# A spectral mixing layer and a two-layer MLP on one core: the PReLU addition one step later, a new step table, another DMA order on GpSimd, and seven-product down blocks in 18 blocks for 21

## The chip, the core and the metric

The kernel runs on one core of a Trainium2 chip. The metric is the device time of one execution in microseconds (us). Engines are named as the profile names them: PE multiplies matrices, PEld is its weight load, DVE is the vector engine, ACT the scalar engine, POOL is GpSimd (it issues part of the DMAs), SP issues the other DMAs.

## The reference

```python
X = np.fft.rfft(x, axis=1)                     # x: 8 batches x 3008 tokens x 256
y = np.fft.irfft(X * (filt_r + 1j * filt_i)[None], n=3008, axis=1)
x = y.reshape(24064, 256)
h = x @ w_in                                   # 256 -> 2048
g = np.maximum(h, 0.0) + alpha * np.minimum(h, 0.0)
out = g @ w_out                                # 2048 -> 256
```

A filter in the frequency domain mixes the tokens of each batch; then every token goes through a two-layer MLP with a PReLU whose slope is given per hidden unit.

## The kernel before, in words

**The transform.** 3008 is 47 x 64. Each batch's transform is made of four kinds of pieces, all matmuls on PE in float16. `piece_a` (16 per batch, L209) is the first stage over 47; its results are evicted into `asb`, a buffer of 384 KB (two of them), and every fourth piece saves one to a scratch tensor in DRAM (`a_dram`, L214, on SP). `turn_a` (L221, SP) loads it back transposed as `at`. `piece_b` (12 per batch, each a pair of frequencies, L229) is the second stage, and DVE multiplies its PSUM result by two forms of the filter, `ww` (with `filts_s`, L232) and `uu` (with `filt_s`, L233); a pair of DMAs on POOL (L235) adds `ww` into `uu` with the two halves of the partitions exchanged. `piece_c` (12, L247) starts the inverse from `uu`; its results go out to `v_dram` and come back as `zt` (L256, L265, SP). `piece_d` (16, L272) ends the inverse and is evicted into `yT`, where the MLP reads it. Batch zero has its own form of these pieces (class First) without the detours through DRAM, and it runs mostly before the steps begin; its last pieces are `piece_t` and `piece_d`. All the transform's PSUM results share two banks, `psF0` and `psF1`, in an order that the string BANKS writes out.

**The MLP.** The 24064 tokens are cut into 48 blocks (512 tokens, every twelfth-from-sixth 384). A block has 16 **steps**; step 16n + j is step j of block n. In a step, `up` (L497) makes one of 16 slices of the hidden layer: two matmuls into half of a two-bank PSUM tile `hps`, of which there are two. In each odd step the tile is full: ACT copies it into `gtb` (L505, 128 x 1024), DVE makes min(g, 0) times (alpha - 1) in two instructions (L508, into `m`), and adds `m` to `gtb` (L509). `gtb` has room for two blocks.

**The down product** of a block follows its up products by LAG steps, interleaved with the next blocks' ups: `while todo and done < (step - LAG) / 16` draws its matmuls. It has two forms. `eight` (L534) is the plain product: 64 matmuls of 256 columns for 512 tokens, evicted by ACT (L539). `seven` (L556), for the blocks in FAST, is a Strassen-Winograd product of 2 x 2 blocks: 112 matmuls of 128 columns. It needs sums of parts of `g`, made in two halves each (`sums`): w = 1 and w = 2 on DVE into `ss` (L517, L519), w = 3 and w = 4 as adding DMAs on POOL within `gtb` (L521, `gtb<-gtb`) and from `ss` (L523, `gtb<-ss`); SUMS and TAIL give the steps, counted from the block's first. It has five evictions on ACT and two additions on DVE (L476, through the list `late`). Combinations of `w_out` for it are made once (`combine`, STEPS_K).

**The order.** No scheduler moves anything: each engine runs its instructions in the order in which the program issues them, and semaphores hold it where data or buffers are missing. The tables say at which step a piece is issued, in steps from a batch's origin, 96 (b - 1): STEPS_A to STEPS_D for batches four to seven, FIRST for batches one to three, STEPS_T and STEPS_E for the rest of batch zero, STEPS_X for loading x of batches two and three, STEPS_N for the four negations of `filt_s` (`neg`, L623). A step number so orders the instructions of one engine; an engine that has nothing to wait for runs ahead of the others. Within a step come: the late additions and stores, the sums, the planned pieces, `up`, and the down matmuls that are due.

**POOL's queue at the opening** (L434 to L441): w_out in two DMAs, x of batch one in eight, one copy of `twi_s`, two copies of half of `filt_s` into `filts_s` (768 KB each), and then batch two's x as its step and its buffers allow.

Of the kernel before, what the change touches and what calls it, by code (L numbers as in the profile page):

```python
# [19 lines left out]
DFF = 2048  # L20
NH = 32
BANKS = (
    "010101010101010101010101010101001010010110010010101010101010101010110101101010101010101011010101"
    "010101010101010101010110110101001011010101011010110111010010101010101010010110100010101110101101"
    "010010101100101010010101010101010101001101010101010010110111010110101010101010101010101010101001"
    "010101010100101101101010010101010101010101010101010101100101101010110100100010100101010101010101"
    "01010101010101101010101101001110101010101010101010101010"
)
STEPS_A = (-84, -81, -77, -76, -65, -59, -58, -58, -56, -53, -52, -51, -50, -48, -46, -43)
STEPS_B = (-21, -15, 4, 6, 13, 21, 25, 27, 32, 40, 54, 55)  # L30
STEPS_C = (2, 10, 16, 19, 24, 33, 35, 46, 62, 63, 70, 70)
STEPS_D = (89, 89, 90, 91, 92, 94, 95, 98, 100, 101, 105, 113, 118, 125, 144, 147)
STEPS_T = (0, 0, 2, 2, 13, 17, 19, 21, 21, 35, 40, 43)
STEPS_E = (6, 6, 7, 11, 23, 27, 29, 29, 53, 54, 55, 56)
STEPS_N = (24, 29, 35, 37)
STEPS_K = (118, 121, 128, 133, 143)
STEPS_X = ((20, 27, 42, 52), (107, 109, 113, 126))
FIRST = (
# [12 lines left out]
)  # L51
FAST = frozenset((8, 10, 12, 14, 16, 18, 20, 22, 24, 26, 28, 30, 32, 34, 36, 38, 40, 42, 43, 44, 45))
SUMS = ((9, 1, 0), (10, 3, 0), (16, 2, 0), (17, 1, 1), (17, 3, 1), (19, 2, 1), (20, 4, 0), (21, 4, 1))
TAIL = ((12, 1, 0), (12, 3, 0), (18, 1, 1), (18, 3, 1), (18, 2, 0), (18, 2, 1), (20, 4, 0), (21, 4, 1))
LAG = 16
AF = mybir.ActivationFunctionType
OP = mybir.AluOpType

# [41 lines left out]
def kernel(  # L100
# [10 lines left out]
    nc = tc.nc  # L111
# [30 lines left out]
    twi_s = konst.tile([128, NK1, 128], FP16, name="twi_s")  # L142
    filt_s = konst.tile([128, NK1, D], FP16, name="filt_s")
    filts_s = konst.tile([128, NK1, D], FP16, name="filts_s")
# [12 lines left out]
    twx_s = tw_s.rearrange("p a k c -> p (a k) c")[:, 0:NK1]  # L157
    yT = konst.tile([128, 2, 2 * NFFT], FP16, name="yT")

    def xrow(b, h, c):  # L160
        return bass.AP(tensor=x.tensor, offset=x.offset + (b * NFFT + NH * h + 8 * c) * D,
                       ap=[[N2 * D, N1], [1, 8 * D]])

    def load_x(b, c):
        xs = p_x.tile([2 * N1, 8 * D], FP16, name="xs")
        for h in range(2):
            nc.gpsimd.dma_start(out=xs[h * N1 : h * N1 + N1], in_=xrow(b, h, c))  # L167
        return xs
# [187 lines left out]
    xc = {(0, c): load_x(0, c) for c in range(4)}  # L356
# [15 lines left out]
    def both_halves(eng, ka, kb):  # L372
        eng.tensor_copy(twi_s[64:128, ka:kb], twi_s[0:64, ka:kb])
        eng.tensor_copy(twx_s[0:64, ka:kb], twx_s[64:128, ka:kb])
# [12 lines left out]
    def warm(n):  # L387
        pw = obank()
        for _ in range(n):
            nc.tensor.matmul(pw[:, 0, 0:128], id16, id16, start=True, stop=True)  # L390
# [27 lines left out]
    for kp in range(12):  # L418
        if kp == 9:
            f0.piece_c(8, on_act)  # L420
        if kp < 10:
            if kp == 3:
                both_halves(nc.vector, 4, 8)
            f0.piece_b(kp + 2)
        if kp < 8:
            f0.turn_at(kp + 4, on_act)
        if kp == 0:
            load_twi(12, 24, on_act)
            both_halves(nc.gpsimd, 12, 18)
            both_halves(nc.gpsimd, 18, 24)  # L430
        for k in range(max(kp - 2, 0), kp - 1) if kp < 8 else (6, 7) if kp == 8 else (kp,):
            f0.piece_c(k, on_act)
    for q in range(2):
        nc.gpsimd.dma_start(  # L434
            out=wout_s[:, 8 * q : 8 * q + 8],
            in_=moe_w_out[1024 * q : 1024 * q + 1024].rearrange("(j p) d -> p j d", p=128))
    for c in range(4):
        xc[(1, c)] = load_x(1, c)
    nc.gpsimd.dma_start(out=twi_s[64:128], in_=twx_s[64:128])
    for o in (0, 64):  # L440
        nc.gpsimd.dma_start(out=filts_s[o : o + 64], in_=filt_s[64:128])  # L441
    warm(8)
    for i in range(4):
        f0.piece_t(i, both[i % 2], i % 2 == 1)
# [34 lines left out]
    class Block:  # L479
        def __init__(self, n, p, t0, tn):  # L480
            self.n, self.p, self.t0, self.tn = n, p, t0, tn
            self.fast = n in FAST
            self.sent = 0
# [8 lines left out]
        def up(self, j):  # L492
            tn = self.tn
            if j % 2 == 0:
                self.hps = psH.tile([128, 2, 512], FP32, name="hps")
            for kt in range(2):
                nc.tensor.matmul(self.hps[:, j % 2, 0:tn], win_s[:, kt, j * 128 : (j + 1) * 128],  # L497
                                 yT[:, kt, self.t0 : self.t0 + tn], start=(kt == 0), stop=(kt == 1))
            if j % 2 == 1:
                g = self.pair(j // 2)  # L500
                m = p_m.tile([128, 2, 512], FP16, name="m")
                hs, ms = self.hps[:, :, 0:tn], m[:, :, 0:tn]
                if self.fast:
                    hs, ms = (t.rearrange("p l (h c) -> p l h c", h=2) for t in (hs, ms))
                nc.scalar.activation(g, hs, AF.Copy)  # L505
                for i in range(2):
                    a = alm_s[:, j - 1 + i : j + i]
                    nc.vector.tensor_scalar(ms[:, i], g[:, i], 0.0, a, OP.min, OP.mult)  # L508
                nc.vector.tensor_add(g, g, ms)  # L509

        def sums(self, w, h):
            k = slice(4 * h, 4 * h + 4)
# [101 lines left out]
    def put(step, fn, *args):  # L614
        plan.setdefault(step, []).append((fn, args))

    for i in range(12):
        ev = both[i % 2] if i < 4 else (on_dve, on_act)[i // 8]
        put(STEPS_T[i], f0.piece_t, 4 + i, ev)
        put(STEPS_E[i], f0.piece_d, 4 + i, ev)  # L620

    def neg(ka, kb):
        nc.vector.tensor_scalar(filt_s[64:128, ka:kb], filt_s[0:64, ka:kb], -1.0, None, OP.mult)  # L623

    for i in range(4):
        put(STEPS_N[i], neg, 6 * i, 6 * i + 6)
    for b in range(1, NB):
        p = 96 * (b - 1)
        f = Fft(b)
        steps_a, steps_b, steps_c, steps_d = FIRST[b - 1] if b < 4 else (STEPS_A, STEPS_B, STEPS_C, STEPS_D)  # L630
        for i in range(16):
# [3 lines left out]
        if b + 1 < NB:  # L635
            for c in range(4):
                put(STEPS_X[b - 1][c] if b < 3 else p - 8 + 4 * c,
                    lambda b=b, c=c: xc.update({(b + 1, c): load_x(b + 1, c)}))
# [27 lines left out]

    for n in range(5):
        put(STEPS_K[n], combine, n)
    blk, todo, ahead = Block(-2, 0, 0, 0), [], {}
    done = 0.0  # L670
    for n, (p, t0, tn, _) in enumerate(blocks):
        old, blk = blk, Block(n, p, t0, tn)
        if blk.fast:
            for at, w, h in SUMS if n < 39 and n - 1 not in FAST else TAIL:
                ahead.setdefault(16 * n + at, []).append((blk, w, h))
        for j in range(16):
            step = 16 * n + j
            flush()
            for b, w, h in ahead.pop(step, ()):
                assert w > 2 or not old.fast or b is old or old.sent >= 88 - 16 * w + 8 * h  # L680
                b.sums(w, h)
            for fn, args in plan.pop(step, ()):
                fn(*args)
            blk.up(j)
            while todo and done < (step - LAG) / 16:
                try:
                    done += next(todo[0])
                except StopIteration:
                    todo.pop(0)
        todo.append(blk.items())  # L690
    for it in todo[:-1]:
        for _ in it:
            pass
# [33 lines left out]
```

## Time and profile before

| | |
|---|---|
| runs, us | 783.4, 784.0, 786.46; median 784.0 |
| profiled execution, us | 781.17 (span of its instructions 779.1) |
| granted clock of PE | 1.00 |
| steps begin, us from the span's start | 37.2 |
| block 0 (steps 0 to 15), us | 37.2 to 49.4 |
| block 1, us | 49.4 to 71.5 |
| blocks 2 to 46, us each | 12.7 to 18.2 |
| DMA: packets, MB, mean rate | 114959, 122.93 MB, 158 GB/s |

The span is the time from the first to the last instruction of one execution; the runs' times are those of whole executions, a little longer. Blocks are longer where many pieces of the transform fall into them. PE's granted clock is the share of its full speed. An engine's line in a timeline gives start, duration, engine, source line, operation, the tile written and those read, the shape, how many were merged, and in brackets the idle time before it and what ended it. A line of waits gives who waited, for whom, total us, times, longest us. In the DMA views q0 is the queue that POOL feeds and q1 that of SP; columns are packets, MB, and the share of sixteen engines' time.

### The profile page before, as it was taken

How to read it: one execution, taken by the hardware profiler on the slowest of the kernel's cores; microseconds unless marked ns; L12 is line 12 of the kernel's file. 1: busy time of each engine (PE TensorE's matmuls, PEld its weight loads, DVE VectorE, ACT ScalarE, POOL GpSimd, SP SyncE). 2: the span in 40 equal slices, each digit the busy share in tenths (PEclk: the TensorE clock that was granted, in tenths of full speed). 3: DMA queues.
4: the chain of work that ended last, by engine and by line, in shares of the span. 5: the costliest groups of instructions: out<-in, count | busy, mean ns of one | idle time of the engine just before them, and what ended most of it. 6: DMA issues, size and time to landing. Idle time of an engine off the chain costs nothing.

```text
span 779.1 us, 18298 instructions
## 1 busy us (share of the span) xinstructions
PE 759.0 (97%) x6952; PEld 540.7 (69%) x6952; DVE 687.3 (88%) x1501; ACT 605.1 (78%) x902; POOL 273.4 (35%) x361
## 2 busy tenths in 40 slices
PE   7898999999999999999999999999999999999998
PEld 6755667666677767766667767767667777777766
DVE  4786996799999999899899989989899999889994
ACT  4687778888878887788868887788878777787763
POOL 7720542144244341453324423434223434102210
PEclk9999999999999999999999999999999999999999
DMA  9994868766997779975799769886797555735642
GB/s 192 187 224 121 163 121 189 207 123 146 198 211 169 147 152 199 214 164 122 163 215 190 147 136 196 197 169 130 162 204 171 109 116 95 181 86 110 121 96 68
DMA packets 114959, 122.93 MB, mean 158 GB/s; under 512 B 12776, under 2 KB 94456, under 8 KB 114744
## 3 DMA queue, kind: packets, MB, share of 16 engines
q0 software_dynamic: 34736, 52.19, 40.8%
q1 hardware_dynamic: 79992, 69.52, 33.4%
q8 instruction: 54, 0.88, 0.5%
q14 instruction: 33, 0.27, 0.1%
q10 hardware_dynamic: 144, 0.07, 0.0%
HBM read 56.06 MB, written 46.66 MB: 132 GB/s over the span
## 4 chain that ended last, share of the span: by engine, by line
PE 80%; DVE 7%; DMA 7%; ACT 3%; issue 2%; POOL 1%; DVEq 0%; ACTq 0%; POOLq 0%
PE hps L497 36%; PE op L534 20%; PE op L556 14%; PE psF L209 3%; DMA gtb<-ss 3%; PE psF L272 2%; PE psF L247 2%; PE psF L229 2%; DVE m L508 2%; DVE gtb L509 2%; ACT gtb L505 2%; DMA a_dram<-asb 1%; DMA filt_s<-in_filt_r_dram 1%; DVE ww L232 1%; DVE uu L233 1%
## 5 line engine op out<-in xcount | busy, mean ns | idle before, releaser
L505 ACT ACTIVATE gtb<-hps 128x1024 f16<-128x1024 f32 (+1 forms) x384 | 386.3, 1006 | 104.4 <-PE hps L497 101.9
L497 PE MATMUL hps<-yT,win_s 128*128 128x512 f16 (+1 forms) x1536 | 449.2, 374 | 0.0
L508 DVE TENSOR_SCALAR m<-gtb,alm_s 128x512 f16<-128x512 f16 (+1 forms) x768 | 235.6, 349 | 48.5 <-ACT gtb L505 46.5
L509 DVE TENSOR_TENSOR gtb<-gtb,m 128x1024 f16<-128x1024 f16 (+1 forms) x384 | 261.6, 681 | 17.2
L534 PE MATMUL op<-wout_s,gtb 128*128 128x256 f16 x1600 | 243.3, 272 | 0.0
L534 PEld LDWEIGHTS <-gtb 128*128 128x128 f16 x1600 | 156.1, 98 | 105.1
L235 POOL DMA_DIRECT2D uu<-ww x168 | 141.1, 1038 | 246.9 <-DVE uu L233 125.2
L497 PEld LDWEIGHTS <-win_s 128*128 128x128 f16 x1536 | 136.6, 98 | 25.7 <-issue 2.7
L556 PEld LDWEIGHTS <-gtb 128*128 128x128 f16 x1680 | 114.4, 98 | 55.1 <-DMA gtb<-ss 2.5
L521 POOL DMA_DIRECT2D gtb<-gtb x42 | 41.8, 994 | 193.7 <-DVE ss L517 74.3
L556 PE MATMUL op<-wout_s,gtb 128*128 128x128 f16 x1008 | 85.6, 219 | 2.3 <-DMA gtb<-ss 1.7
L279 ACT ACTIVATE asb<-psF 96x512 f16<-96x512 f32 x112 | 65.4, 594 | 14.5 <-PE psF L209 10.8
L279 ACT ACTIVATE yT<-psF 128x376 f16<-128x376 f32 x120 | 57.0, 488 | 11.0 <-PE psF L272 10.3
L556 PEld LDWEIGHTS <-ss 128*128 128x128 f16 x672 | 47.1, 98 | 23.3
L556 PE MATMUL op<-tw_s,gtb 128*128 128x128 f16 x672 | 58.0, 219 | 0.0
L556 PE MATMUL op<-tw_s,ss 128*128 128x128 f16 x672 | 58.0, 219 | 0.0
L232 DVE TENSOR_TENSOR ww<-psF,filts_s 128x512 f16<-128x512 f32 x84 | 57.4, 683 | 0.0
L233 DVE TENSOR_TENSOR uu<-psF,filt_s 128x512 f16<-128x512 f32 x84 | 57.2, 681 | 0.0
L279 ACT ACTIVATE v<-psF 128x512 f16<-128x512 f32 x84 | 49.7, 598 | 8.7 <-PE psF L247 7.9
L167 POOL DMA_DIRECT2D xs<-in_x_dram x64 | 41.4, 969 | 23.6 <-PE psF L209 11.7
L523 POOL DMA_DIRECT2D gtb<-ss x42 | 45.2, 1264 | 4.7 <-PE op L556 2.4
L272 PE MATMUL psF<-wi_s,zt 96*128 96x94 f16 x504 | 39.6, 205 | 4.4 <-ACT asb L279 3.1
(85 smaller groups left out, 517.8 us busy)
## 6 DMA issues: line engine op xcount, KB each, us to landing
out_dram<-osb SPq DMA_DIRECT2D x127, 128.0 KB
xs<-in_x_dram POOLq DMA_DIRECT2D x64, 188.0 KB, 7.5
a_dram<-asb SPq DMA_DIRECT2D x28, 384.0 KB
uu<-ww POOLq DMA_DIRECT2D x168, 64.0 KB, 3.2
v_dram<-v SPq DMA_DIRECT2D x112, 96.0 KB
zt<-v_dram SPq DMA_DIRECT2D x28, 384.0 KB
gtb<-gtb POOLq DMA_DIRECT2D x42, 256.0 KB, 4.0
gtb<-ss POOLq DMA_DIRECT2D x42, 256.0 KB, 5.9
```

The costliest lines, as they stand in the source:

```text
L232: nc.vector.tensor_mul(ww, px, filts_s[:, 2 * kp : 2 * kp + 2])
L233: nc.vector.tensor_mul(uu, px, filt_s[:, 2 * kp : 2 * kp + 2])
L235: nc.gpsimd.dma_start(out=uu[o : o + 64], in_=ww[64 - o : 128 - o], accum_op=OP.add)
L272: nc.tensor.matmul(ps[:, m], self.zt[g][:, 4 * mh + m, dh * 128 : dh * 128 + 128], wi3_s, start=True, stop=True)
L279: nc.scalar.activation(o, i, AF.Copy)
L497: nc.tensor.matmul(self.hps[:, j % 2, 0:tn], win_s[:, kt, j * 128 : (j + 1) * 128], yT[:, kt, self.t0 : self.t0 + tn], start=(kt == 0), st ...
L505: nc.scalar.activation(g, hs, AF.Copy)
L508: nc.vector.tensor_scalar(ms[:, i], g[:, i], 0.0, a, OP.min, OP.mult)
L509: nc.vector.tensor_add(g, g, ms)
L523: nc.gpsimd.dma_start(out=a12, in_=z2, accum_op=OP.add)
L534: nc.tensor.matmul(op[:, si % 2], self.pair(k // 2)[:, k % 2, 128 * si : 128 * si + 128], wout_s[:, k], start=(k == 0), stop=(k == 15))
L556: nc.tensor.matmul(acc[:, 128 * i : 128 * i + 128], x[:, k, 128 * i : 128 * i + 128], b[:, k], start=first and k + i == 0, stop=k == 7, sk ...
```

## The change

The addition that ends the PReLU is no longer issued with its two scales. It goes on a list, `owed`, and is issued in the next step, behind that step's late additions, sums and planned pieces and ahead of its `up`. LAG grows from 16 to 17.25. The seven-product form is used in 18 blocks (9, 11, 13, 15, every even one from 18 to 42, and 45) for 21, and its sums have new steps. All tables of steps, and BANKS, are new. On POOL, batch one's x goes ahead of w_out; the copy of `twi_s` is issued at step 1, and the two large filter copies become eight of a quarter each, in pairs at steps 5, 15, 33 and 53.

```diff
-STEPS_A = (-84, -81, -77, -76, -65, -59, -58, -58, -56, -53, -52, -51, -50, -48, -46, -43)
-STEPS_B = (-21, -15, 4, 6, 13, 21, 25, 27, 32, 40, 54, 55)
-STEPS_C = (2, 10, 16, 19, 24, 33, 35, 46, 62, 63, 70, 70)
+STEPS_A = (-82, -81, -80, -78, -68, -60, -58, -57, -56, -55, -54, -51, -50, -48, -45, -45)
+STEPS_B = (-19, -15, 2, 6, 11, 22, 24, 29, 34, 46, 59, 59)
+STEPS_C = (2, 12, 17, 20, 22, 33, 42, 57, 64, 67, 68, 69)
-STEPS_N = (24, 29, 35, 37)
+STEPS_N = (15, 27, 48, 58)
+STEPS_F = (1, 5, 15, 33, 53)
-STEPS_X = ((20, 27, 42, 52), (107, 109, 113, 126))
+STEPS_X = ((24, 24, 68, 79), (85, 86, 88, 98))
 FIRST = (
-    ((8, 10, 15, 16, 16, 17, 19, 20, 22, 22, 24, 25, 26, 28, 28, 30),
-     (41, 41, 45, 45, 49, 54, 58, 63, 65, 65, 71, 72),
-     (48, 50, 52, 58, 60, 62, 69, 70, 71, 73, 77, 80),
+    ((5, 11, 13, 17, 17, 17, 19, 20, 22, 23, 23, 24, 26, 27, 28, 28),
+     (39, 42, 42, 46, 52, 54, 57, 60, 63, 63, 68, 72),
+     (48, 50, 52, 59, 60, 61, 67, 68, 71, 71, 78, 80),
...
-FAST = frozenset((8, 10, 12, 14, 16, 18, 20, 22, 24, 26, 28, 30, 32, 34, 36, 38, 40, 42, 43, 44, 45))
-SUMS = ((9, 1, 0), (10, 3, 0), (16, 2, 0), (17, 1, 1), (17, 3, 1), (19, 2, 1), (20, 4, 0), (21, 4, 1))
-TAIL = ((12, 1, 0), (12, 3, 0), (18, 1, 1), (18, 3, 1), (18, 2, 0), (18, 2, 1), (20, 4, 0), (21, 4, 1))
-LAG = 16
+FAST = frozenset((9, 11, 13, 15, 18, 20, 22, 24, 26, 28, 30, 32, 34, 36, 38, 40, 42, 45))
+SUMS = ((12, 1, 0), (12, 3, 0), (18, 1, 1), (20, 2, 0), (20, 2, 1), (22, 3, 1), (22, 4, 0), (22, 4, 1))
+TAIL = ((9, 1, 0), (11, 3, 0), (17, 2, 0), (21, 1, 1), (22, 2, 1), (23, 4, 0), (25, 3, 1), (31, 4, 1))
+LAG = 17.25
...
+    for c in range(4):
+        xc[(1, c)] = load_x(1, c)
     for q in range(2):
         nc.gpsimd.dma_start(
             out=wout_s[:, 8 * q : 8 * q + 8],
             in_=moe_w_out[1024 * q : 1024 * q + 1024].rearrange("(j p) d -> p j d", p=128))
-    for c in range(4):
-        xc[(1, c)] = load_x(1, c)
-    nc.gpsimd.dma_start(out=twi_s[64:128], in_=twx_s[64:128])
-    for o in (0, 64):
-        nc.gpsimd.dma_start(out=filts_s[o : o + 64], in_=filt_s[64:128])
...
-                nc.vector.tensor_add(g, g, ms)
+                owed.append((g, ms))
...
+    def swapped(ka, kb):
+        for o in (0, 64):
+            nc.gpsimd.dma_start(out=filts_s[o : o + 64, ka:kb], in_=filt_s[64:128, ka:kb])
+
+    put(STEPS_F[0], lambda: nc.gpsimd.dma_start(out=twi_s[64:128], in_=twx_s[64:128]))
     for i in range(4):
+        put(STEPS_F[1 + i], swapped, 6 * i, 6 * i + 6)
         put(STEPS_N[i], neg, 6 * i, 6 * i + 6)
...
+    owed = []
+
+    def settle():
+        for g, ms in owed:
+            nc.vector.tensor_add(g, g, ms)
+        owed.clear()
+
...
             for fn, args in plan.pop(step, ()):
                 fn(*args)
+            settle()
             blk.up(j)
...
         todo.append(blk.items())
+    settle()
```

The tables that are not shown (STEPS_D, STEPS_T, STEPS_E, STEPS_K, the fourth row of FIRST's first batch and its rows for batches two and three, and BANKS) move in the same way, by a few steps.

More of the change, by code (lines that the diff above doesn't have):

```diff
@@ L22 @@
 BANKS = (
[L23 to L27, printed above, removed]
-)
-STEPS_A = (-84, -81, -77, -76, -65, -59, -58, -58, -56, -53, -52, -51, -50, -48, -46, -43)
@@ L30 @@
-STEPS_B = (-21, -15, 4, 6, 13, 21, 25, 27, 32, 40, 54, 55)
-STEPS_C = (2, 10, 16, 19, 24, 33, 35, 46, 62, 63, 70, 70)
-STEPS_D = (89, 89, 90, 91, 92, 94, 95, 98, 100, 101, 105, 113, 118, 125, 144, 147)
-STEPS_T = (0, 0, 2, 2, 13, 17, 19, 21, 21, 35, 40, 43)
-STEPS_E = (6, 6, 7, 11, 23, 27, 29, 29, 53, 54, 55, 56)
-STEPS_N = (24, 29, 35, 37)
-STEPS_K = (118, 121, 128, 133, 143)
-STEPS_X = ((20, 27, 42, 52), (107, 109, 113, 126))
-FIRST = (
[12 rows of a table removed]
-)
-FAST = frozenset((8, 10, 12, 14, 16, 18, 20, 22, 24, 26, 28, 30, 32, 34, 36, 38, 40, 42, 43, 44, 45))
@@ L53 @@
-SUMS = ((9, 1, 0), (10, 3, 0), (16, 2, 0), (17, 1, 1), (17, 3, 1), (19, 2, 1), (20, 4, 0), (21, 4, 1))
-TAIL = ((12, 1, 0), (12, 3, 0), (18, 1, 1), (18, 3, 1), (18, 2, 0), (18, 2, 1), (20, 4, 0), (21, 4, 1))
-LAG = 16
+    "010101010101010101010101010100101001101010010010100110101010010100101011010010110101010100101010"
+    "101010101010101010101001010101001010101101010101001010110101010101010101010101001101010101010110"
+    "101010110101001001010101010101010101011011010101010010100101010101011010101010101010101010101011"
@@ new lines @@
+    "011010101010101001001010101001010101010101010101010101001001010101010101101101010101101010101010"
+    "10101010101010110110101010110101010101010101010101010101"
+)
+STEPS_A = (-82, -81, -80, -78, -68, -60, -58, -57, -56, -55, -54, -51, -50, -48, -45, -45)
+STEPS_B = (-19, -15, 2, 6, 11, 22, 24, 29, 34, 46, 59, 59)
+STEPS_C = (2, 12, 17, 20, 22, 33, 42, 57, 64, 67, 68, 69)
+STEPS_D = (88, 88, 91, 92, 93, 94, 94, 96, 97, 103, 106, 115, 117, 126, 145, 148)
+STEPS_T = (0, 0, 3, 3, 12, 14, 18, 21, 21, 32, 40, 45)
@@ new lines @@
+STEPS_E = (6, 6, 9, 10, 24, 26, 29, 30, 51, 55, 57, 58)
+STEPS_N = (15, 27, 48, 58)
+STEPS_F = (1, 5, 15, 33, 53)
+STEPS_K = (115, 124, 126, 127, 162)
+STEPS_X = ((24, 24, 68, 79), (85, 86, 88, 98))
+FIRST = (
[12 rows of a table added]
+)
+FAST = frozenset((9, 11, 13, 15, 18, 20, 22, 24, 26, 28, 30, 32, 34, 36, 38, 40, 42, 45))
+SUMS = ((12, 1, 0), (12, 3, 0), (18, 1, 1), (20, 2, 0), (20, 2, 1), (22, 3, 1), (22, 4, 0), (22, 4, 1))
+TAIL = ((9, 1, 0), (11, 3, 0), (17, 2, 0), (21, 1, 1), (22, 2, 1), (23, 4, 0), (25, 3, 1), (31, 4, 1))
@@ L680 @@
                 assert w > 2 or not old.fast or b is old or old.sent >= 88 - 16 * w + 8 * h
+                assert not (owed and b is blk and h == (j - 1) // 8)
                 b.sums(w, h)
```

18 rows, old and new, of the table FIRST are left out of this document.

## The prediction

> **What bounds the kernel now.** I read the page's engine totals first, then the chain, then what PE waited for, then the stretches in which it waited.
>
> ```profile
> span 779.1 us, 18298 instructions
> PE 759.0 (97%) x6952; PEld 540.7 (69%) x6952; DVE 687.3 (88%) x1501; ACT 605.1 (78%) x902; POOL 273.4 (35%) x361
> PEclk9999999999999999999999999999999999999999
> PE 80%; DVE 7%; DMA 7%; ACT 3%; issue 2%; POOL 1%; DVEq 0%; ACTq 0%; POOLq 0%
> ```
>
> PE is busy 97% and holds 80% of the chain, at the full granted clock (1.00). Busy is not peak, so I take the distance between starts. These rows of PE's timeline are a step with an eight-product block behind it, and one with a seven-product block:
>
> ```profile
> 300.88 0.60 PE L534 MATMUL op<-wout_s,gtb 128*128 128x256 f16 x4
> 301.31 0.59 PE L497 MATMUL hps<-yT,win_s 128*128 128x512 f16 x2
> ```
> ```profile
> 320.94 0.55 PE L556 MATMUL op<-tw_s,gtb 128*128 128x128 f16 x7
> 321.33 0.49 PE L497 MATMUL hps<-yT,win_s 128*128 128x384 f16 x2
> ```
>
> Four products of 256 columns take 0.43 us (109 ns each), seven of 128 take 0.39 us (56 ns each); two of 512 columns take 0.43 us (216 ns each). I subtracted these distances from every gap between PE starts. What is left over is PE's lost time: 27.3 us of the span. 10.7 us of it lie ahead of 37.2 us, where the steps begin and where the change touches nothing on PE; 2.9 us in block 0 (37.2 to 49.4), 4.6 in block 1 (to 71.5), 0.5 and 1.2 in blocks 2 and 3, and 7.3 in the blocks behind them. So a new order can win at most 16.5 us, half of it in the first two blocks. What PE waited for:
>
> ```profile
> PE psF L272 <- ACT asb L279: 3.1, 1, 3.1
> ...
> PE op L556 <- DMA gtb<-ss: 1.7, 2, 1.0
> PE psF L247 <- DMA uu<-ww: 1.0, 1, 1.0
> ```
>
> The largest is one wait of 3.1 us at 61 us, and ACT's timeline shows where it is from:
>
> ```profile
> 60.37 1.08 ACT L279 ACTIVATE asb<-psF 96x512 f16<-96x512 f32 x2 [3.04 <-DMA a_dram<-asb]
> ```
>
> ACT stood because batch one's first save (384 KB, issued 49.93) had not left its buffer. The DMA view of 50 to 54 us says why, and that of 56 to 60 us when it ended:
>
> ```profile
> q0 software_dynamic: 92, 0.88, 103.2%
> q1 hardware_dynamic: 5, 0.02, 1.5%
> ```
> ```profile
> q0 software_dynamic: 175, 0.52, 65.9%
> q1 hardware_dynamic: 150, 0.55, 35.4%
> ```
>
> POOL's queue (q0) held the engines with w_out, x and the two filter copies of 768 KB (landing 52.9 and 56.6); the save on SP's queue (q1) moved 0.02 MB in 4 us.
>
> **The change, part by part.**
>
> *Seven products in 18 blocks for 21.* Per block 64 x 109 - 112 x 56 = 704 ns more on PE; three blocks: **+2.1 us**, all on the path. DVE loses 3 x 6 additions of 0.685 us (12.3 us), ACT 3 x (5 x 0.387 - 2 x 0.60) = 2.2 us, POOL 12 DMAs of about 1.1 us: all beside PE.
>
> *Addition a step later.* 384 additions of 0.69 us as before. DVE now takes sums, filter products and evictions first. PE waited for an addition (L509) 0.5 us in all, so the gain is at most 0.5; what is behind the late addition is the down product, which LAG 17.25 moves by 1.25 steps too. LAG costs those 1.25 steps in the opening, where PE lost 2.9 us in 16 steps: 1.25 x 0.18 = **+0.2**. At the end it only moves work: 0. DVE's 46.5 us of waits for ACT were never PE's.
>
> *x ahead of w_out, copies in parts.* In POOL's order of the changed program the queue is x (8), w_out (2), the twi copy, four quarter copies, then batch two's x (4), and the other four parts behind. POOL runs ahead of the steps until it reaches batch two's x, which needs a buffer that PE frees at step 17. So half of the copies, 768 KB, leaves the backlog: 3.6 us at the 3.7 us that the second copy took after the first (52.88 to 56.60). The backlog then ends near 50.5 us instead of 54. The six more DMAs cost POOL 6 x 0.53 us, in its idle time. w_out lands some 8 us later, near 48 us; it is first read at step 18, past 52: 0.
> But the save is issued at step 17 instead of 16 and its buffer is wanted at step 22 (piece 8): 5 steps, about 5.3 us, where it had 7. Uncontested saves of later batches landed in 3.0 to 3.6 us, the contested second one here in 7.8. So the wait of 3.0 us becomes 0 (first row) to 2.5 (second); I take 0.5, nearer to the first, as the backlog is gone: **-2.5**.
> [...]
>
> *Steps, the opening.* PE's other waits in blocks 0 and 1 are 7.5 - 3.2 = 4.3 us, for PSUM banks that ACT or DVE had not emptied (0.73, 0.58, 0.40, 0.65 the largest). Batch one's pieces at steps 15, 16 and 16 move to 11, 13 and 17; three at 17 then meet. I take a quarter off, **-1.1** (0 to -3). The first negation, now at step 15, must wait for two quarter copies (landing near 50.7 by the backlog above): DVE may stand 1.5 us there. Behind it stand the scales of step 15 and an eviction of step 18; down products read them from step 21 on, so 0 (to +1.5).
>
> *Steps, batch one's filter products.* The 1.0 us wait at 92.4 had 7 steps from product to use; that pair now has 10. But pair 5 has 7 steps, about 7.8 us, behind the last copy in POOL's queue, and took 7.5: **-0.4** (-1.1 to +1.5).
>
> *Steps, batches four to seven.* Pairs 10 and 11 stood at steps 53 and 54 and were used at 70. Now both stand at 59 and are used at 68 and 69: 5 x 0.964 + 4 x 0.906 = 8.4 us and 9.3 us (blocks 21 and 22 took 15.42 and 14.50 us). From PE's product to the landed addition of `uu` pair 10 took 7.0, 8.9, 9.0 and 7.2 us, and pair 11 11.7, 12.2, 10.7 and 8.7. The long ones fell into the next batch's load of `at`; batch seven has none behind it.
>
> ```profile
> 384.99 2.85 SPq L221 DMA_DIRECT2D at<-a_dram  x4
> ```
> ```profile
> 382.75 3.40 POOL L235 DMA_DIRECT2D uu<-ww  x4 [3.69 <-DVE uu L233]
> ```
> ```profile
> DMA to landing us min/median/max: 2.7/3.4/7.2
> ```
>
> (SP's timeline, POOL's, and `uu` in 378 to 394 us.) The load's last part landed at 394.7, ten us after its first issue. It moves 2 steps earlier, the pairs 5 to 6 later, so they are issued in its second half. Late by 0 (rows of 7.0) to 3.1 (mean of 11.7, 12.2, 10.7, less 8.4) in each of three batches. I take 0.5, near the short end, because half the load is through by then: **+1.5** (0 to +9.4).
>
> *Steps, sums of the seven-product blocks.* PE lost 3.4 us to them in 21 blocks; 18/21 of that: **-0.5**. Their DMAs follow the DVE sums, 1.5 to 1.7 steps later than before, for products 1.25 steps later: slack falls by up to 0.4 us, where it was 0.05 us in three blocks and 1 to 5 us in most (0 to +3; -3.4 if all go).
>
> **Sum.** 2.1 + 0.2 - 2.5 - 1.1 - 0.4 + 1.5 - 0.5 = -0.7 us against the profiled execution's 781.2 us (span 779.1): 780.5. The median of the runs shown is 784.0, 2.8 us above that execution, so **783** as a median.
>
> **Rivals.**
> *Faster: the new placing removes most of what PE lost.* Openings of 7.5 us fall to 1.5, the `uu` waits to 0, the sums' to 1: 2.1 - 6.0 - 1.0 - 2.4 = -7.3, so 776.7. For it: the two POOL edits sit exactly on the largest wait, and the other 44 blocks show an order can run with almost no loss (0.35 us in 510 to 700). Against it: the 4.3 us of bank waits came where pieces met in one step, and the new steps 17 to 24 hold eight of batch one's.
> *Slower: the `at` load meets pairs 10 and 11.* Their additions queue for the full 3.1 us in batches four, five and six: -0.7 - 1.5 + 9.4 = +7.2, so 791. It decides once an addition lands over 8.4 us after its product. For it: pair 11's three rows. Against it: the load moves ahead two steps.
> *The opening's gain does not come.* Batch two's x goes out at the very step of the first save and keeps its landing at the 10.4 us of before, with two steps (1.9 us) fewer: the wait grows by 1.9 instead of falling by 2.5, so -0.7 + 2.5 + 1.9 = +3.7 and 787.7. For it: in the 56 to 60 us rows q0 still moved as much as q1. Against it: there the first save got through at once. [...]
>
> **How the numbers follow.** Forecast 0.40, faster rival 0.33, `at` rival 0.17, opening rival 0.10. A difference under 0.5% (3.9 us) is about what a measurement of this kernel can not tell from no change. Faster by more: the faster rival and a little of the forecast's edge, 0.35. Slower by more: the `at` rival, half of the opening rival and an edge, 0.25. Same: 0.40. The range takes in both outer rivals with a margin: 774 to 792; the forecast's own is 779 to 787.
>
> **What would show it.** 704 ns x 3 more PE issue time. The first save landing within 5.3 us, and no ACT wait for it over 1 us. PE's waits for `uu` at steps 68 and 69 of batches four to six at most 0.5 us each, with the landings beside them. DVE's wait at the first negation not passed on to PE. The prediction is wrong if PE's loss in blocks 0 and 1 stays near 7.5 us, if the `uu` waits exceed 1 us a batch, or if a wait appears on a queue not named here.

## The result, and the profile after

The changed kernel is slower: 791.5 us median over 19 runs (785.4 to 795.6), against 786.3 for the kernel before in as many runs on the same chip; the ratio is 1.0064, with a 95% interval of 1.0045 to 1.0082. The forecast was 783 beside 784.0 (a ratio of 0.999), so a small gain where a loss clear of the noise came out; the rival "the `at` load meets pairs 10 and 11" had said 791.

The page of the changed kernel, the same totals and the chain as were shown of before:

```profile
span 789.5 us, 18030 instructions
PE 762.3 (97%) x6808; PEld 541.1 (69%) x6808; DVE 670.0 (85%) x1483; ACT 603.3 (76%) x893; POOL 267.2 (34%) x355
PE 84%; DMA 7%; DVE 3%; ACT 3%; POOL 2%; issue 1%; DVEq 0%; SPq 0%; POOLq 0%; ACTq 0%
```

The span grew by 10.4 us (the profiled execution took 791.3). PE still bounds it, and DVE and ACT have less to do than before, as the diff says; so the loss isn't work on another engine. Taking PE's gaps apart as the prediction did (distance between starts, less the matmul's own 216, 109 or 56 ns) gives 2.11 us more of issue time (the matmuls of each kernel, counted at these distances) and 8.42 us more of lost time; the 0.1 us that this is above the span's growth lies ahead of the first matmul:

| PE's lost time, us | before | after |
|---|---|---|
| ahead of the steps | 10.74 | 10.51 |
| blocks 0 and 1 | 7.46 | 4.03 |
| blocks 2 to 5 | 2.21 | 3.25 |
| blocks 6 to 17 | 3.52 | 3.13 |
| blocks 18 to 41 | 2.26 | 14.75 |
| blocks 42 to 47 | 1.08 | 0.02 |
| sum | 27.27 | 35.69 |

The opening won what it was to win, and blocks 18 to 41, where the change was priced at a microsecond or two, lost 12.5 us more. What PE waited for after the change (total us, times, longest):

```profile
PE psF L248 <- DMA uu<-ww: 8.1, 3, 3.2
...
PE op L554 <- ACT osb L568: 2.3, 1, 2.3
...
PE psF L273 <- DMA zt<-v_dram: 1.7, 1, 1.7
...
PE psF L230 <- DMA v_dram<-v: 1.0, 1, 1.0
```

Line 248 is `piece_c`. The three waits stand at 391.0, 487.4 and 579.7 us: step 68 of batches four, five and six, pair 10 each time, and none in batch seven, behind which no load follows. The 3.1 us wait on L272 for ACT, the largest of before, is gone. PE's timeline at the first of the three, and the stretches that follow each (us of PE, PEld, DVE, ACT and POOL busy, then PE's granted clock, DMA share, GB/s):

```profile
391.00 0.38 PE L248 MATMUL psF<-uu,twi_s 128*128 128x256 f16 x2 [3.17 <-DMA uu<-ww]
391.21 0.59 PE L495 MATMUL hps<-yT,win_s 128*128 128x512 f16 x2
391.64 0.75 PE L532 MATMUL op<-wout_s,gtb 128*128 128x256 f16 x4
392.18 0.64 PE L248 MATMUL psF<-uu,twi_s 128*128 128x256 f16 x2
392.61 0.63 PE L495 MATMUL hps<-yT,win_s 128*128 128x512 f16 x1
```
```profile
390.60:396.00 5.40, 5.00 (x24) 3.00 (x25) 1.46 (x4) 2.22 (x3) 0.00 (x0) 0.68 0.72 198
...
487.00:492.00 5.00, 4.61 (x33) 3.21 (x34) 2.78 (x7) 3.05 (x4) 0.00 (x0) 1.00 0.61 159
...
579.40:585.00 5.60, 5.28 (x26) 3.15 (x27) 0.97 (x3) 2.22 (x3) 0.00 (x0) 0.70 0.65 162
```

Behind the two waits of 3 us and more the granted clock is 0.68 and 0.70 for some 5 us, and starts lie twice as far apart for a stretch of it (granted clock 0.50 from 392.0 to 395.3 us and from 579.8 to 583.0): the two products at 391.00 take 0.21 us, the two at 392.18 take 0.43. Behind the third wait the clock is 1.00. By the distances of PE's starts, which count 0.16 us more for a wait than the page does, the waits are 3.3, 2.1 and 3.2 us, and the slow clock costs 1.7 and 1.6 us. So pairs 10 and 11 cost 3.3 + 2.1 + 3.2 = 8.6 us of waiting and 3.3 us of slow clock, 11.9 of the 14.75 us; the wait for `osb` at 692 us is 2.5 more.

Why the additions are late is seen on SP's timeline, on POOL's, and in the DMA queues from 383 to 390.6 us (packets, MB, share of the sixteen engines' time):

```profile
380.14 3.30 SPq L222 DMA_DIRECT2D at<-a_dram  x4
```
```profile
382.35 3.34 POOL L236 DMA_DIRECT2D uu<-ww  x4 [4.32 <-DVE uu L234]
```
```profile
q1 hardware_dynamic: 2683, 1.41, 96.2%
q0 software_dynamic: 318, 0.26, 22.5%
```

The four additions are issued 2.2 us behind the load's first part, and share the engines with it until it has landed at 390.6. They landed 6.7 to 8.0 us after their issue, where the same four took 2.3 to 3.4 us in batch seven. Before, the first of the four stood 2.2 us *ahead* of the load (382.75 and 384.99).

In the opening, ACT's row that answers to the 3.04 us one of before:

```profile
57.19 1.08 ACT L280 ACTIVATE asb<-psF 96x512 f16<-96x512 f32 x2 [0.15 <-PE psF L210]
```

The first save, issued at 50.1 us, now landed 4.4 us after its issue (10.35 before), and ACT no longer waited for it.

### The profile page after: what moved, and what is told of

The parts are those of the page before. It is cut to its first block, busy times and chain, and to the rows that moved or that the text cites. A ratio compares the mean times of both kernels' runs of the same rounds, so it can differ in the third digit from the quotient of the medians.

```text
span 789.5 us, 18030 instructions
## 1 busy us (share of the span) xinstructions
PE 762.3 (97%) x6808; PEld 541.1 (69%) x6808; DVE 670.0 (85%) x1483; ACT 603.3 (76%) x893; POOL 267.2 (34%) x355
## 4 chain that ended last, share of the span: by engine, by line
PE 84%; DMA 7%; DVE 3%; ACT 3%; POOL 2%; issue 1%; DVEq 0%; SPq 0%; POOLq 0%; ACTq 0%
PE hps L495 37%; PE op L532 24%; PE op L554 11%; DMA uu<-ww 3%; PE psF L210 3%; PE psF L273 3%; PE psF L248 2%; PE psF L230 2%; ACT gtb L503 1%; DMA gtb<-ss 1%; DMA twf_s<-c_twf 1%; DMA out_dram<-osb 1%; DVE m L506 1%; DVE gtb L677 1%; PE op L587 1%
## 5 line engine op out<-in xcount | busy, mean ns | idle before, releaser
L506 DVE TENSOR_SCALAR m<-gtb,alm_s 128x512 f16<-128x512 f16 (+1 forms) x768 | 238.0, 351 | 80.0 <-ACT gtb L503 78.7
L532 PE MATMUL op<-wout_s,gtb 128*128 128x256 f16 x1792 | 273.6, 273 | 0.0
L519 POOL DMA_DIRECT2D gtb<-gtb x36 | 37.1, 1031 | 171.5 <-DVE m L506 51.5
L554 PE MATMUL op<-wout_s,gtb 128*128 128x128 f16 x864 | 74.6, 219 | 0.9 <-DMA gtb<-ss 0.9
L554 PEld LDWEIGHTS <-ss 128*128 128x128 f16 x576 | 39.7, 98 | 22.7 <-issue 2.4
L554 PE MATMUL op<-tw_s,gtb 128*128 128x128 f16 x576 | 49.9, 219 | 0.4 <-DMA gtb<-gtb 0.4
L554 PE MATMUL op<-tw_s,ss 128*128 128x128 f16 x576 | 47.0, 219 | 2.3 <-ACT osb L568 2.3
L521 POOL DMA_DIRECT2D gtb<-ss x36 | 34.0, 1123 | 34.6 <-DVE m L506 17.4
L210 PE MATMUL psF<-xs,wf_s 94*96 94x512 f16 x112 | 41.1, 381 | 0.6 <-DVE zt L283 0.4
```

The source lines that it names most:

```text
L210: nc.tensor.matmul(ps[0:96], wf1_s, xs[:, o : o + 512], start=True, stop=True)
L532: nc.tensor.matmul(op[:, si % 2], self.pair(k // 2)[:, k % 2, 128 * si : 128 * si + 128], wout_s[:, k], start=(k == 0), stop=(k == 15))
L554: nc.tensor.matmul(acc[:, 128 * i : 128 * i + 128], x[:, k, 128 * i : 128 * i + 128], b[:, k], start=first and k + i == 0, stop=k == 7, sk ...
```

## The experiments

Each ratio is against runs of the kernel before made beside it, whose medians were 784.6 to 787.2 us; experiments 2, 4 and 5 rest on four runs each, the others on nine to twelve, and experiment 10 on one each.

**Theory A:** pairs 10 and 11 lose the time because the next batch's `at` load is in the engines while they are added, and the new steps leave pair 10 8.3 us from product to use. **Rivals:** the additions are late for a reason of their own in the new order (DVE or POOL come to them late, or other stores hold them), or the loss is made of the later addition and the many other moves, with the three waits standing in for them.

**1. The two pairs used later, all else as changed.**

```diff
-STEPS_C = (2, 12, 17, 20, 22, 33, 42, 57, 64, 67, 68, 69)
+STEPS_C = (2, 12, 17, 20, 22, 33, 42, 57, 64, 67, 71, 72)
```

> The changed kernel with one edit: pieces c of pairs 10 and 11 in batches four to seven stand at steps 71 and 72 instead of 68 and 69; nothing else moves on PE. Theory A (the loss is PE waiting for the additions of these two pairs, which the next batch's load of at delays): the three waits of 3.2, 2.0 and 3.1 us go, and with them the stretches of halved clock behind them (about 1.7 us after each of the two long ones), so the time falls by 8 to 11 us against the changed kernel's profile, to a ratio of 0.993 to 0.998 of the kernel before. Rival B (the loss is spread over the new order, and PE waits at the next place when this one is taken away, for instance for the last zt of the same batch): PE's lost time stays within 3 us of the changed kernel's, ratio 1.003 or more.

784.6 us; 0.998 of before (0.995 to 1.001). The span is 780.0, 9.5 us under the changed kernel's. The waits of PE for the additions:

```profile
PE psF L248 <- DMA uu<-ww: 0.7, 1, 0.7
```

The additions landed as late as ever (11.1, 10.9 and 11.7 us after the product for pair 10), only PE hardly stood for them; the clock stayed at 1.00 throughout and blocks 18 to 41 lost 4.55 us for 14.75. Two step numbers carry the loss.

**2. The old steps of the two pairs tightened the same way in the kernel before.**

```diff
-STEPS_B = (-21, -15, 4, 6, 13, 21, 25, 27, 32, 40, 54, 55)
-STEPS_C = (2, 10, 16, 19, 24, 33, 35, 46, 62, 63, 70, 70)
+STEPS_B = (-21, -15, 4, 6, 13, 21, 25, 27, 32, 40, 59, 59)
+STEPS_C = (2, 10, 16, 19, 24, 33, 35, 46, 62, 63, 68, 69)
```

> The kernel before with one edit, the reverse of the undoing: in batches four to seven pairs 10 and 11 move from 53 and 54 to 59, their uses from 70 to 68 and 69. Theory A: it gets the same three waits of 2 to 3.3 us in batches four to six and none in batch seven, with halved clock behind the long ones, and is 7 to 11 us slower than the kernel before in its profile, ratio 1.007 to 1.012. Rival B (the pairs are late in the changed kernel because of other things of the new order, such as the later addition or the sums): under 3 us, ratio below 1.004.

800.7 us, 1.0195 of before (1.017 to 1.022):

```profile
PE psF L247 <- DMA uu<-ww: 12.2, 5, 3.2
```

The waits in batches four to six are 3.3, 3.0 and 3.3 us (none in batch seven) by the distances of starts, and the other two (3.1 us by the page) fall on earlier pairs, at 96 and 210 us. The cause is there without any other part of the change. The loss is larger than either theory had said: blocks 18 to 41 lost 14.9 us as in the changed kernel, and blocks 0 to 17 lost 6.5 us more than in the profile of before, which this experiment doesn't touch. What that is shows in experiment 10.

**3. The load issued later, at step 12 of its list for 4.**

```diff
-        quarters, later = (4, 1) if b < 3 else (1, 4)
+        quarters, later = (4, 1) if b < 3 else (1, 12 if b > 4 else 4)
```

> The changed kernel with one edit: for batches five to seven the load of at is issued 12 steps after the last piece a instead of 4, so behind the additions of pairs 10 and 11 of the batch before; the pairs stay at 59 and their uses at 68 and 69. Theory A (the load is what delays the additions): the additions land 3.1 to 4.5 us after their issue instead of 6.5 to 8.5, PE's waits for them fall under 0.5 us each, time as in the run with later uses. Rival C (9 and 10 steps are too short for the chain of product, two DVE products and adding DMA whatever else moves): waits of over 1 us remain with the load out of the way.

1.0053 of before (1.002 to 1.0086): the changed kernel once more. The eight steps moved the load past no other instruction of SP's queue, SP was ahead of the steps anyway, and the load went out as early as before (waits for `uu` 8.5 us in all). A step number here is a place in a queue, not a time; the experiment tells nothing on A.

**4. The load put behind the next stores on SP's queue.** The same line with 14 for 12.

> The changed kernel with the load of at for batches five to seven put behind the store of v that waits for pair 8 (step 64) in SP's queue, so that it really starts some 5 us later; pairs 10 and 11 stay at 59, their uses at 68 and 69. Theory A (the load delays the additions): they land 3.1 to 4.5 us after their issue instead of 6.5 to 8.5, PE's three waits of 2 to 3.3 us fall to 0.5 or less; the load itself may then be late for the next batch's first product, by up to 2 us. Rival C (9 and 10 steps are too few for this chain in any case): waits of over 1 us remain at the two uses.

800.2 us, 1.0172 (1.014 to 1.020). The load now goes out at 395.35 us, behind four `v` stores, and the additions have the engines to themselves (387 to 391.6 us):

```profile
393.19 2.06 SPq L257 DMA_DIRECT2D v_dram<-v  x4
395.35 2.25 SPq L222 DMA_DIRECT2D at<-a_dram  x4
```
```profile
q0 software_dynamic: 319, 0.26, 42.7%
```

There is no row of q1 in that stretch, the pairs of additions landed 3.2 to 4.7 us after their first issue in batches four to six, where they took 6.5 to 8.5 us in the changed kernel, and no wait for `uu` is left. So the load is what delays them, and the rival with a reason inside the additions falls. But the load has no spare time either; it is the one that is late now, and for longer than I had expected (up to 2 us each):

```profile
PE psF L230 <- DMA at<-a_dram: 12.7, 3, 5.3
```

**5. The addition issued at once, all else as changed.**

```diff
-                owed.append((g, ms))
+                nc.vector.tensor_add(g, g, ms)
```

> The changed kernel with the addition issued at once behind its scales, all else as it is (LAG 17.25). By the prediction the place of the addition is worth nothing: the ratio to the kernel before stays 1.003 to 1.009, as the changed kernel's, and the three waits for pairs 10 and 11 stay within 1 us of theirs. If the later addition helped the pairs by letting their products pass on DVE, the waits grow by about the 0.7 us of an addition each.

806.5 us, 1.0268 of before (1.024 to 1.029), so 2% over the changed kernel. The waits of the two pairs grew to 3.9, 3.3 and 4.6 us, and PE's waits for DVE behind the start of the steps came to 5.4 us (17 times), where the changed kernel has one of 0.4 us:

```profile
PE psF L248 <- DMA uu<-ww: 11.6, 4, 4.5
```

**6. The later addition alone, in the kernel before** (`owed` and `settle` as in the diff, LAG 16 kept).

> The kernel before with the later addition alone (LAG stays 16, all steps as before). By the prediction's step it costs nothing and gains at most 0.5 us: ratio 0.998 to 1.002. Rival: the later addition makes DVE wait longer for ACT or the down products wait for the additions, and carries part of the loss: 1.003 or more, with PE waits named by the addition's line.

1.0008 (0.998 to 1.003). In the old tables the late addition is worth nothing either way; in the new ones taking it away costs 2%. PE's new waits for DVE in experiment 5 are behind filter products and evictions, so the new steps count on DVE being free for these at once. The pairs' longer waits aren't explained so: POOL issued pair 10's additions only 0.2 us later after the product than in the changed kernel, and they took 0.3 to 1.3 us longer to land; why is not shown. Its worth belongs to the tables.

**7. The opening alone, in the kernel before:** the edits of POOL's queue (x ahead of w_out, the copies in parts at steps 1, 5, 15, 33 and 36), old steps.

> The kernel before with the POOL edits alone: batch one's x ahead of w_out, the copy of twi_s at step 1, the filter copies in quarters at steps 5, 15, 33 and 36 (36, for the negation at 37 has to follow it); all other steps as before. If the backlog on POOL's queue is what starved the first save: the save lands in 4 to 6 us, ACT's wait of 3.0 us goes, PE loses 2.5 to 3.5 us less in blocks 0 and 1, ratio 0.995 to 0.998. If the save is held by batch two's x as well: the wait stays over 2 us and the ratio is 0.999 to 1.001.

1.0002 (0.998 to 1.0025). In the profile ACT's 3 us are gone, the first save landed 5.9 us after its issue, and blocks 0 and 1 lost 4.32 us for 7.46: the part did what it was priced at. The time did not move clear of the noise (the interval is some 2 us to either side), and in the profile blocks 18 to 41 lost 6.48 us for 2.26:

```profile
PE op L554 <- DMA gtb<-ss: 4.5, 3, 2.3
```

**8. The two pairs made early again (54 and 55), used at 68 and 69; batch one's first `piece_d` 1 to 2 steps later.**

```diff
-STEPS_B = (-19, -15, 2, 6, 11, 22, 24, 29, 34, 46, 59, 59)
+STEPS_B = (-19, -15, 2, 6, 11, 22, 24, 29, 34, 46, 54, 55)
...
-     (93, 94, 95, 95, 98, 99, 104, 105, 107, 108, 115, 117, 118, 120, 125, 128)),
+     (95, 95, 96, 96, 98, 99, 104, 105, 107, 108, 115, 117, 118, 120, 125, 128)),
```

> The changed kernel with pairs 10 and 11 of batches four to seven at 54 and 55, ahead of the next batch's load of at, and batch one's first four pieces d two steps later, for they waited 1.8 to 3.2 us for zt. Theory A: no wait over 1 us is left at either place, PE loses 22 to 25 us of its span instead of 35.7, span 774 to 778, ratio 0.990 to 0.996. Rival B (a wait taken away comes back at the next place): 0.998 or more.

781.9 us, 0.9955 (0.994 to 0.997): with the two pairs made earlier the changed kernel is faster than before. But they are not all ahead of the load, as I had expected: in batch five the load was issued at 474.10 us and the pairs' additions at 474.79 and 476.58, and they landed 7.1 and 8.6 us later, beside it. So the distance is enough by itself, as in experiment 1: pair 10 now has 13.4 us from product to use for 8.3. The second half missed; `piece_d` came later and still stood, PE lost 27.1 us for the 22 to 25 said, and the span was 780.7:

```profile
PE psF L273 <- DMA zt<-v_dram: 3.1, 1, 3.1
```

**9. Batch three's x put back to steps 107 to 126** (and the pairs of experiment 8, without its `piece_d`).

```diff
-STEPS_X = ((24, 24, 68, 79), (85, 86, 88, 98))
+STEPS_X = ((24, 24, 68, 79), (107, 109, 113, 126))
```

> The changed kernel with two rows of steps put back: pairs 10 and 11 of batches four to seven at steps 54 and 55 for 59 and 59, and batch three's x at steps 107, 109, 113 and 126 for 85, 86, 88 and 98. Theory: batch one's v stores landed late (7.7 us after issue in the changed kernel, about 2 before) because batch three's x loads on POOL's queue run at the same time; with the loads put back the stores land in under 4 us and PE's wait for zt<-v_dram (1.7 us in the changed kernel, about 3.1 in two variants of it) goes below 0.5. Together with the freed uu additions: span 776 to 779 us, time 0.990 to 0.995 of the kernel before. Rival: the v stores are late for a reason inside batch one (the evictions on ACT that fill them come late in the new order); then the wait stays at 1.5 to 3.2 us and the time at 0.995 to 0.998.

781.0 us, 0.994 (0.992 to 0.996). The wait for `zt` is 1.5 us, inside the rival's range, so by its own terms my theory missed, though the span of 779.2 us and the ratio are in its range. But the experiment had moved only one pair of loads: POOL still issued six between 115.0 and 119.6 us. SP's rows of this run, `v` stores and the load of `zt` that waits for them:

```profile
120.83 2.53 SPq L257 DMA_DIRECT2D v_dram<-v  x4
129.33 1.25 SPq L266 DMA_DIRECT2D zt<-v_dram  x3
```

**10. The kernel before, and the opening alone, profiled once more.**

> The kernel before, unchanged, for one more profile. What PE loses by parts should come back as in the profile that the prediction was worked from: about 7.5 us in blocks 0 and 1 with the one wait of 3 us for ACT, 1.7 us in waits for gtb<-ss, span 778 to 781 us. If instead the sum waits come out above 4 us, single profiles of these kernels differ by as much as the opening's gain and can't show where it went.

> The kernel before with the edits of POOL's queue at the opening alone, for one more profile. If the waits for gtb<-ss in blocks 8 to 45 (4.5 us in its first profile, 1.7 in that of the kernel before) are bound to this order, they come back above 4 us and the opening's gain of 3 us is given back there. If they come out near 1.7 us, the first profile was a draw, and the span should be about 3 us below that of the kernel before.

The first: 789.4 us and a span of 787.5, 8.4 us more than the profile that the prediction was worked from, for the same program. Its sum waits are as before (2.0 us); two other things differ.

```profile
PE psF L247 <- DMA uu<-ww: 3.1, 1, 3.1
PE psF L272 <- ACT asb L279: 3.0, 1, 3.0
```

The wait for ACT at 61 us is the old one. What follows it isn't. PE's timeline behind that wait in the first profile of before, and in this one:

```profile
61.17 0.60 PE L497 MATMUL hps<-yT,win_s 128*128 128x512 f16 x2
61.61 0.60 PE L534 MATMUL op<-wout_s,gtb 128*128 128x256 f16 x4
```
```profile
61.55 0.85 PE L497 MATMUL hps<-yT,win_s 128*128 128x512 f16 x2
62.19 1.06 PE L534 MATMUL op<-wout_s,gtb 128*128 128x256 f16 x4
```

From 61.17 to 61.61 is 0.44 us, from 61.55 to 62.19 is 0.64, and the four products behind take 0.86 for 0.44: the clock is halved for some 3 us (granted clock 0.60 from 61.1 to 64.4, 1.00 in the first profile), which costs 9.12 - 7.46 = 1.7 us in blocks 0 and 1. At 96.8 us the same pair that had cost 1.0 us costs 3.1, and the clock halves there too (0.52 from 96.6 to 103.0), at a cost of 2.8 us; blocks 2 to 5 lost 7.44 us for 2.21. So single profiles of this kernel differ by more than the opening's gain. Experiment 2's excess of 6.5 us in blocks 0 to 17 is within that, as these two profiles of one program differ by 7.7 us there; half of it is the clock, which halved behind the waits at 61 and 96 us (1.7 and 1.5 us).

The second: 783.9 us, span 782.0. Blocks 18 to 41 lost 6.36 us again, where both profiles of before have 2.26 and 2.49. Its sum waits, at 2.6 us, are between the two values that I had set:

```profile
PE op L554 <- DMA gtb<-ss: 2.6, 2, 1.3
```

So the give-back came back with this order, two profiles against two; more than half of it is such waits. In block 22 the addition of w = 3 is issued at step 21.8 in both profiles of the opening alone and at 20.4 in both of before, though DVE and ACT stand at the same steps to a tenth of one; the sums' last DMA then lands at step 32.0, where PE wants it, and not at 30.3. The trace names an `up` of PE as what POOL waited for in both profiles of the opening alone, and a down product in both of before. Why that differs, 340 us behind the edit, stays open.

**11. Batch two's x put back too.**

```diff
-STEPS_X = ((24, 24, 68, 79), (107, 109, 113, 126))
+STEPS_X = ((24, 24, 42, 52), (107, 109, 113, 126))
```

> The kernel of the run before with the other row of x put back too: the third and fourth part of batch two's x at steps 42 and 52 for 68 and 79. Putting batch three's row back alone had moved only one pair of loads, since POOL runs ahead of the steps: six x loads of 188 KB still went out at 115.0 to 119.6 us, and the v stores issued at 120.8 to 122.9 landed only near 129. With this row back four x loads are left in that stretch and none at 106 us. If x loads hold the v stores, the stores land some 2 to 3 us earlier and PE's wait for zt<-v_dram falls from 1.5 to under 0.5 us: span 777 to 778.5, time 0.990 to 0.994 of the kernel before. Rival: the stores queue behind the 384 KB save of batch two's asb, issued 1 us ahead of them on SP's own queue; then the wait stays at 1 to 2 us, and x loads among batch one's uu additions may cost up to 1 us there: 0.993 to 0.997.

778.8 us, 0.9916 (0.989 to 0.994), the fastest kernel of the study, ahead of the kernel before and of the changed one. SP's rows again, then PE's wait at batch one's second pair:

```profile
123.24 2.73 SPq L257 DMA_DIRECT2D v_dram<-v  x4
129.17 1.25 SPq L266 DMA_DIRECT2D zt<-v_dram  x3
```
```profile
PE psF L248 <- DMA uu<-ww: 2.0, 1, 2.0
```

From the first `v` store to the load that waits for all four: 5.9 us, where it was 8.5 with six x loads ahead (8.8 in the changed kernel, 3.7 before). No wait for `zt` is left. The save on SP's own queue went out 1.4 us ahead of the stores in both, and the last x load landed 1.2 to 1.3 us ahead of the load of `zt` in both, so by these two runs the x loads are what held the stores; that the four loads left still cost 2 us is likely but was not tried. The price stands at batch one's second pair, which now has x beside it and costs PE 2.0 us, and 1.6 us of halved clock behind that; the rival had said up to 1. So everything behind it runs later: the load of `zt` went out at the same 129 us as in experiment 9, and PE came to it 1.9 us later. Blocks 2 to 5 lost 4.8 us for 3.0, so the place of the edit lost time in this profile; its shorter span (777.9 us for 779.2) is from other parts, and against experiment 9 the intervals overlap. That this edit gains anything is not shown.

## Why the prediction was wrong

**Right, and by its own numbers.** PE's issue time: +2.1 said, +2.11 by the count of matmuls. The opening, +0.2 - 2.5 - 1.1 = -3.4 said: blocks 0 and 1 fell from 7.46 to 4.03 us, -3.4; the first save landed in 4.4 us, within the 5.3 set. PE's wait for `asb` fell by 2.5 us and the rest of the two blocks by 0.9, so the parts fit too; that they fit to a tenth is partly luck. Batch one's `uu` wait of 1.0 us is gone (-0.4 said). The sums' waits on PE fell by about 1.6 us for the 0.5 said, with three blocks fewer and another order of the rest. DVE stood 0.9 us at the first negation (1.5 said), and no wait of PE names it.

**The step that failed** is "steps, batches four to seven", the term of +1.5 with bounds of 0 to 9.4. It measured 11.9 us: 3.3, 2.1 and 3.2 us of waits, and 3.3 us of halved clock behind two of them. Two readings in it were wrong:

- "They are issued in its second half ... half the load is through by then." I had added the steps that the pairs and the load move and taken the sum for a time. Both issues hang on data, not on the step: POOL waits for DVE's `uu`, SP for the save. (The count was off too: by the table the pairs moved from 54 and 55, so by 5 and 4 steps, not 5 to 6.) In batch four the additions moved from 2.2 us ahead of the load to 2.2 us behind it, and shared the engines with 8 us of it. Experiment 3 shows the same from the other side: eight steps more moved the load not at all.
- The rows of 7.0 and 7.2 us, to which I put the value nearest, were additions that had hardly any of the load beside them: the first of their batch to be issued, ahead of it (landed 1.0 us behind the load's issue), or in batch seven. The three long rows of pair 11 were the right ones. Given those, the rival comes out, and its place, its three batches and its 3.1 us were right; its chance of 0.17 rested on the wrong rows. That its 791 met the median is partly luck: the kernel before came out at 786.3 and not 784.0, so the loss was 5.2 us for the rival's 7.2, and the slow clock was in neither sum.

What the sum did not hold at all: a wait of 3 us may be followed by a slow clock. The granted clock of 1.00 in the profile of before had let me pass over it, though its one such wait was a case that could go either way (experiment 10), and a clock of 1.00 is not the usual one: of the 17 runs of the kernel before beside experiment 9, three have a clock of 1.00 and took 781.2 to 784.4 us, where the median is 787.2. Of the changed kernel's 19 runs, the two at 1.00 took 785.4 and 786.4 us, and the five at 0.991 or less 793.1 to 795.6. Of the 32 waits of PE of over 1.9 us that the steps of all these kernels' profiles hold, the clock halved behind all six of 3.8 us or more, behind nine of the fifteen between 3.0 and 3.4, behind three of the ten between 2.1 and 2.8, and not behind the one below that; a stretch cost 1.3 to 1.8 us, two of them 2.6 and 2.8. So the length of a wait from 2.1 to 3.4 us doesn't settle it, and one program falls on both sides (the wait of 3 us at 61 us, experiment 10); what settles it there is not shown.

**Named as signs, and seen:** the prediction was to be wrong if the `uu` waits exceeded 1 us a batch, or a wait appeared on a queue not named; both happened. The unnamed ones are `zt` behind `v` stores (1.7 us, x loads moved into their time; experiments 9 and 11), and the eviction L568 that stood 2.7 us for the landing of an `out` store (2.3 us on PE; not tried by itself, and it is gone in experiments 8, 9 and 11).

**Priced at nothing, and not nothing:** the place of the addition. It is worth nothing in the old tables (experiment 6) and 2% in the new (experiment 5), where DVE's filter products and evictions must not stand behind an addition. The two parts can't be priced apart.

## What to carry to other kernels

A DMA's slack is to be priced by rows in which the transfer that will be beside it is beside it, here 6.5 to 9.6 us for 3.1, and not by the median. A step in such a table is a place in a queue; what will overlap is found from what each issue waits for. And a wait of PE from some 2 us on may be followed by a slow clock that costs 1.3 to 1.8 us more here, sometimes 2.8, and was so in all six cases of 3.8 us or more; so it is the first to remove, and two profiles of one program may differ by it.

## What the runs showed of the hardware

- A pair of 64 KB additions issued by POOL landed 3.1 to 3.2 us after the first issue with the engines free (one pair of batch seven in every profile), and 6.5 to 9.6 us beside the `at` load of four times 384 KB (the changed kernel and experiments 1, 2, 3 and 5). In the changed kernel, from 383 to 390.6 us, q1, mostly the load, took 96.2% of the engines' time for 1.41 MB, with 2683 packets for q0's 318. By these rows a packet took 0.962 x 7.6 x 16 / 2683 = 0.044 us on q1 and 0.225 x 7.6 x 16 / 318 = 0.086 on q0. The four additions of batch four took 3.7 to 5.4 us longer than the same four of batch seven, without the load; how the engines divide their time between the two queues is not shown.
- The same program gave spans of 779.1 and 787.5 us, with the clock halved after none of its waits in the first and after two in the second.
